# A fused attention and two-layer MLP kernel: the bank of the filling products is used as two halves of 256 columns

## The chip, the core and the metric

The kernel runs on one core of a Trainium2 chip. The metric is device time in microseconds (us) of one execution. TensorE is called PE, VectorE DVE, ScalarE ACT, GpSimd POOL; SyncE (SP) only starts transfers. PE multiplies a weight tile of 128x128 with a moving tile and adds the result up in PSUM, which has eight banks of 512 float32 columns per partition. ACT and DVE can read PSUM, POOL works on SBUF alone.

## The reference

Three steps follow each other, all in float32:

```
scores = q @ k^T / 8                      # 4 batches x 8 heads, 576 x 576, head size 64
scores = where(scores >= max - tau, scores, -1e9)
x = softmax(scores) @ v                   # gives x: 2304 tokens x 512
g = s * relu(x @ w_in)^2 + b              # w_in 512 x 2048
y = g @ w_out                             # w_out 2048 x 512
h = y @ w2_in                             # second layer, 512 x 2048
out = (max(h,0) + alpha * min(h,0)) @ w2_out
```

## The kernel before

A product of two float32 tiles is made of three fast products: each operand is split in a high and a low part, and `mm3` (lines 504 to 507) issues low x high, high x low and high x high into the same columns of PSUM. So every small step of the first layer is three matmuls, on lines 505, 506 and 507.

The work has four stages: attention (32 heads in 16 pairs), the first layer, and the two products of the second layer. A planner (class `Plan`) takes all tasks with their engine, an estimated time, the buffers that they take and a rank, runs through them in estimated time and writes each engine's instructions in the order that comes out. On the chip that order is fixed: an engine that meets an instruction whose input or buffer is not ready stands there, whatever lies behind it. The waits themselves are put in by the framework below the planner, from what each instruction reads and writes.

Attention leaves PE with gaps. They are filled with a part of the first layer, called the fill here: six blocks of 256 tokens, and of the 16 feature chunks of 128 the first 10 (`NA`). The fill has the lowest rank (`LATER + j`), so the planner issues three of its matmuls when no task of attention is ready. For one block the fill does this (lines 1011 to 1031):

- `load_x` reads 256 tokens of x back from memory and splits them (lines 518 to 524). A block waits here until attention has stored these tokens.
- `hidden` (lines 529 to 538) makes two feature chunks, 2 x 4 x 3 matmuls into the 512 columns of one bank.
- `square` (lines 540 to 558): ACT evicts the bank with a ReLU (line 543), then DVE (lines 548, 549) or POOL (551, 552) squares, ACT makes the high part (555), DVE or POOL the low one (556).
- After five such pairs come the outputs: two output chunks side by side in one bank, 2 x 10 x 3 matmuls, evicted by one ACT copy (line 1028) and stored to `ya`.

Of the eight banks, attention holds two double banks for scores (`sc`) and three single ones (`bank0` to `bank2`). The fourth single bank, `bank3`, is the fill's only one (`moe_s`, line 365); at the start the transposes of the first four pairs use it too (line 681). While a bank is being evicted the planner gives it to nobody, and issues tasks of attention on PE.

When attention has ended, `switch` (line 1036) frees its banks. What is left of the fill and then all other blocks of the first layer (six blocks of 384 tokens, `blocks_b`, lines 1086 to 1126) use them. That next stage starts on PE with products of the tile `xb`, which ACT and DVE make from x (lines 522 and 523).

## Time and profile before

| what | value |
|---|---|
| three timed runs | 1107.9, 1107.91, 1109.72 us; median 1107.91 |
| the profiled execution | 1105.83 us, its span 1104.0 us |
| PE busy | 1072.1 us, 97% of the span |
| DVE busy | 924.6 us, 84% |
| ACT busy | 749.3 us, 68% |
| POOL busy | 341.5 us, 31% |
| granted clock of PE | 0.997 of full speed over the span |

The span runs from the first to the last instruction. Attention and the fill take the first 507 us, and from there PE does the rest of the first layer and the second layer with hardly a gap. Matmuls overlap: one of 256 columns is shown with 0.28 us from start to end, but the next starts 0.12 us after it. So a short wait of PE does not show as idle time in full, and the starts tell more than the busy time.

### The profile page before, as it was taken

How to read it: one execution, taken by the hardware profiler on the slowest of the kernel's cores; microseconds unless marked ns; L12 is line 12 of the kernel's file. 1: busy time of each engine (PE TensorE's matmuls, PEld its weight loads, DVE VectorE, ACT ScalarE, POOL GpSimd, SP SyncE). 2: the span in 40 equal slices, each digit the busy share in tenths (PEclk: the TensorE clock that was granted, in tenths of full speed). 3: DMA queues.
4: the chain of work that ended last, by engine and by line, in shares of the span. 5: the costliest groups of instructions: out<-in, count | busy, mean ns of one | idle time of the engine just before them, and what ended most of it. 6: DMA issues, size and time to landing. Idle time of an engine off the chain costs nothing.

```text
span 1104.0 us, 22088 instructions
## 1 busy us (share of the span) xinstructions
PE 1072.1 (97%) x7536; PEld 1032.0 (93%) x7536; DVE 924.6 (84%) x2076; ACT 749.3 (68%) x1727; POOL 341.5 (31%) x466
## 2 busy tenths in 40 slices
PE   8899999999999999999999999999999999999998
PEld 6677889997999999989999999999999999999998
DVE  4899998989888889868877789589987999998882
ACT  4788877777868878754553467367787998565551
POOL 1466754544756647410000013010120332112111
PEclk8999999999999999999999999999999999999999
DMA  5646365436435453225376555348844474653531
GB/s 129 158 125 178 91 143 129 110 104 152 120 91 129 105 137 91 70 102 163 115 218 212 173 190 165 121 128 269 278 145 162 150 227 140 163 162 111 148 97 39
DMA packets 185264, 158.35 MB, mean 143 GB/s; under 512 B 72000, under 2 KB 162112, under 8 KB 185152
## 3 DMA queue, kind: packets, MB, share of 16 engines
q1 hardware_dynamic: 182624, 154.79, 49.2%
q10 hardware_dynamic: 2528, 2.16, 0.7%
q8 instruction: 59, 0.97, 0.4%
q14 instruction: 53, 0.43, 0.1%
HBM read 91.10 MB, written 44.56 MB: 123 GB/s over the span
## 4 chain that ended last, share of the span: by engine, by line
PE 75%; DVE 11%; ACT 5%; DMA 4%; issue 2%; SPq 1%; POOL 0%; DVEq 0%; ACTq 0%
PE bank L505 11%; PE bank L506 11%; PE bank L507 11%; PE bank_b L506 8%; PE bank_b L507 8%; PE bank_b L505 8%; PE bank L877 6%; PE sc L767 6%; PE bank L298 3%; PE bank L296 3%; DVE e L783 2%; DVE mx L777 1%; ACT e L781 1%; DMA stg<-xs 1%; SPq L645 1%
## 5 line engine op out<-in xcount | busy, mean ns | idle before, releaser
L783 DVE SCALAR_TENSOR_TENSOR e<-sc,mx,e 128x576 f32<-128x576 f32 x144 | 116.1, 812 | 13.0 <-ACT e L781 8.0
L781 ACT ACTIVATE e<-sc,mx 128x576 f32<-128x576 f32 x144 | 106.2, 742 | 19.5 <-DVE mx L777 19.0
L777 DVE TENSOR_REDUCE mx<-sc 128x1 f32<-128x576 f32 x144 | 106.8, 750 | 11.4 <-PE sc L767 10.6
L505 PE MATMUL bank<-gt,wa 128*128 128x256 f32 (+1 forms) x367 | 115.7, 315 | 0.5 <-ACT xr L1198 0.4
L506 PE MATMUL bank<-gt,wa 128*128 128x256 f32 (+1 forms) x367 | 110.3, 300 | 0.3 <-DVE gt L556 0.3
L507 PE MATMUL bank<-gt,wa 128*128 128x256 f32 (+1 forms) x367 | 110.3, 300 | 0.0
L298 PE MATMUL bank<-eyes,e 128*128 128x128 f32 (+1 forms) x320 | 90.3, 288 | 2.0 <-DVE e L783 1.9
L505 PE MATMUL bank<-xt,wa 128*128 128x256 f32 (+1 forms) x262 | 81.4, 311 | 3.8 <-ACT rest L543 3.2
L506 PE MATMUL bank<-xt,wa 128*128 128x256 f32 (+1 forms) x262 | 75.1, 287 | 0.0
L507 PE MATMUL bank<-xt,wa 128*128 128x256 f32 (+1 forms) x262 | 75.0, 286 | 0.0
L779 POOL TENSOR_SCALAR mx<-mx,tau_s 128x1 f32<-128x1 f32 x144 | 47.5, 331 | 81.8 <-DVE mx L777 78.3
L505 PEld LDWEIGHTS bank<-gt,wa 128*128 128x128 f32 x367 | 70.4, 192 | 1.2 <-ACT xr L1198 0.7
L506 PEld LDWEIGHTS bank<-gt,wa 128*128 128x128 f32 x367 | 69.5, 189 | 0.5 <-DVE gt L556 0.5
L507 PEld LDWEIGHTS bank<-gt,wa 128*128 128x128 f32 x367 | 69.4, 189 | 0.0
L767 PE MATMUL sc<-k,q 128*128 128x288 f32 x272 | 66.6, 371 | 2.7 <-DVE e L783 2.2
L877 PE MATMUL bank<-gl,vt 128*128 128x256 f32 (+1 forms) x192 | 63.6, 332 | 0.9 <-DVE gl L935 0.8
L877 PE MATMUL bank<-gh,vt 128*128 128x256 f32 (+1 forms) x192 | 57.9, 302 | 1.3 <-DVE gl L943 0.4
L505 PEld LDWEIGHTS bank<-xt,wa 128*128 128x128 f32 x262 | 50.6, 193 | 5.7 <-ACT rest L543 4.4
L767 PEld LDWEIGHTS sc<-k,q 128*128 128x128 f32 x272 | 44.9, 195 | 10.3 <-DVE e L783 3.8
L935 DVE TENSOR_TENSOR gl<-bank,gh 128x256 fp32r<-128x256 f32 (+1 forms) x96 | 43.3, 451 | 12.7 <-ACT gh L933 12.2
L566 ACT ACTIVATE gt<-rest,b_b,s_b 128x384 fp32r<-128x384 f32 x56 | 39.3, 705 | 21.0 <-DVE rest L564 20.6
L563 ACT ACTIVATE rest<-bank_b 128x384 f32<-128x384 f32 x39 | 19.1, 490 | 50.7 <-PE bank_b L507 50.6
(675 smaller groups left out, 4176.8 us busy)
## 6 DMA issues: line engine op xcount, KB each, us to landing
stg<-in_moe_w_in_dram SPq DMA_DIRECT2D x32, 512.0 KB, 4.1
stg<-in_moe_w_out_dram SPq DMA_DIRECT2D x32, 512.0 KB, 3.8
qo<-hq SPq DMA_DIRECT2D x32, 256.0 KB, 4.5
gf<-rest SPq DMA_DIRECT2D x34, 192.0 KB, 2.0
rest<-gf SPq DMA_DIRECT2D x46, 128.0 KB, 2.8
ko<-hk SPq DMA_DIRECT2D x32, 144.0 KB, 2.5
xr<-xs SPq DMA_DIRECT2D x6, 768.0 KB, 4.5
yf<-yb SPq DMA_DIRECT2D x24, 192.0 KB, 2.7
```

The source lines that it names most:

```text
L298: nc.tensor.transpose(to, part(x), one)
L505: nc.tensor.matmul(o, lhsT=wl, rhs=mh, start=first, stop=False, skip_group_check=on_top)
L506: nc.tensor.matmul(o, lhsT=wh, rhs=ml, start=False, stop=False, skip_group_check=on_top)
L507: nc.tensor.matmul(o, lhsT=wh, rhs=mh, start=False, stop=last, skip_group_check=on_top)
L566: t = add("ACT", act(n, 2, True), lambda: nc.scalar.activation(g.t[:, 0, :n], r.t[:, :n], AF.Identity, bias=b_b, scale=s_b), (r,), (g,), r ...
L767: nc.tensor.matmul(sp.t[:, x, :HS], lhsT=o[0][:, c], rhs=o[1][:, x * HS:(x + 1) * HS], start=n == 0, stop=n == len(passes) - 1)
L777: add("DVE", dve(S), lambda sp=sp, mx=mx: nc.vector.tensor_reduce(mx.t[:, 0:1], sp.t[:, :, :HS], op=ALU.max, axis=AX.XY, negate=True), (sp ...
L779: t2 = add("POOL", 0.26, lambda mx=mx: nc.gpsimd.tensor_scalar(mx.t[:, 1:2], mx.t[:, 0:1], -1.0, tau_s, op0=ALU.mult, op1=ALU.subtract), ( ...
L781: add("ACT", act(S, 1), lambda sp=sp, mx=mx, e=e: nc.scalar.activation(halves(e.t), sp.t[:, :, :HS], AF.Exp, bias=mx.t[:, 0:1]), (sp, mx), ...
L783: add("DVE", dve(S) + 0.065, lambda sp=sp, mx=mx, e=e, col=col, sums=sums: nc.vector.scalar_tensor_tensor(halves(e.t), sp.t[:, :, :HS], mx ...
L877: nc.tensor.matmul(o.t[:, :n], lhsT=w.rearrange("p a b -> p (a b)"), rhs=m.t[:, :n], start=c == first and x == 0, stop=c == last and x == ...
L935: add("DVE", dve(n), lambda hi=hi, lo=lo, gt=gt: nc.vector.tensor_tensor(lo.t[:, :n], gt.t[:, :n], f32(hi.t[:, :n]), op=ALU.subtract), (gt ...
```

## The change

The fill no longer takes `bank3` as a whole. When the last transposes of the first four pairs have been evicted, the bank is handed over as two halves of 256 columns (`half_s`), and from then on they stay with the fill until its end. A half holds one feature chunk of one block, or one output chunk. Each half is evicted by its own ACT instruction of 256 columns; the squaring that follows still works on two chunks at once. The first product of a block now comes after the last product of the block before (`full` is set behind each pair of output chunks). The banks that attention leaves go to the next stage alone, which gets `bank3` when the fill has ended.

```diff
--- before.py
+++ after.py
@@ -362,7 +362,8 @@
     banks = tiles(ps, 4, "bank", [P, 512])
     two_s = Slots(tiles(ps_att, 2, "sc", [P, 2, 512]))
     one_s = Slots(banks[:3], {"gt": 2, "o": 1, "misc": 1})
-    moe_s = Slots(banks[3:], {"h": 1})
+    whole_s, half_s, moe_s = Slots(banks[3:]), Slots(), Slots(caps={"h": 4})
+    of_whole = []
 
     def hwdge(fn, reads=(), writes=(), rank=None, kb=128, after=()):
         return add("SP", 0.6, fn, reads, writes, after, rank, tail=Plan.LAND + kb / 180.0)
@@ -526,21 +527,22 @@
         chain[0] = (t,)
         return xs
 
-    def hidden(xs, n, fs, units, rank, last=()):
-
-        h = Buf(moe_s, "h")
-        for i, f in enumerate(fs):
-            u = units[f // 2]
-            for c, x in enumerate(xs):
-                def go(i=i, f=f, c=c, x=x, u=u):
-                    mm3(h.t[:, i * n:(i + 1) * n], u.w_in(0, c, f), u.w_in(1, c, f), x.t[:, 0], x.t[:, 1], c == 0, c == NC - 1)
-                last = (add("PE", pe_r(n, 3), go, (x, u.buf), (h,), after=last, rank=rank),)
+    def hidden(xs, n, f, units, rank, last, slots):
+
+        h = Buf(slots, "h")
+        u = units[f // 2]
+        for c, x in enumerate(xs):
+            def go(c=c, x=x):
+                mm3(h.t[:, :n], u.w_in(0, c, f), u.w_in(1, c, f), x.t[:, 0], x.t[:, 1], c == 0, c == NC - 1)
+            last = (add("PE", pe_r(n, 3), go, (x, u.buf), (h,), after=last, rank=rank),)
         return h, last[0]
 
-    def square(h, n, r_slots, g_slots, others):
-
+    def square(hs, m, r_slots, g_slots, others):
+
+        n = m * len(hs)
         r, g = Buf(r_slots), Buf(g_slots)
-        add("ACT", act(n), lambda: nc.scalar.activation(r.t[:, :n], h.t[:, :n], AF.Relu), (h,), (r,), rank=SOON)
+        for i, h in enumerate(hs):
+            add("ACT", act(m), lambda i=i, h=h: nc.scalar.activation(r.t[:, i * m:(i + 1) * m], h.t[:, :m], AF.Relu), (h,), (r,), rank=SOON)
 
         def go(e):
             x = r.t[:, :n]
@@ -678,7 +680,7 @@
                     if s0:
                         tr = of_tails
                     else:
-                        tr = Buf(one_s, {"k": "misc", "q": "gt"}[nm]) if p == 0 and not tail else Buf(moe_s) if whole else Buf(one_s, "misc")
+                        tr = Buf(one_s, {"k": "misc", "q": "gt"}[nm]) if p == 0 and not tail else Buf(whole_s) if whole else Buf(one_s, "misc")
 
                         def transpose(t=t, tr=tr, cs=(NQ,) if tail else tuple(range(NQ))):
                             for i, c in enumerate(cs):
@@ -692,6 +694,7 @@
                         if nm == "k":
                             add("ACT", act(n), lambda hl=hl, tr=tr, c=c, n=n: nc.scalar.activation(
                                 k32[p][:, c], tr.t[:, :n], AF.Copy), (tr,), (hl,), rank=ready)
+                            of_whole.append(plan.tasks[-1])
                             continue
                         for h in range(2):
                             c0 = 2 * NQ * P + h * TL if tail else h * NQ * P
@@ -703,6 +706,7 @@
                                     nc.scalar.activation(q32[p][:, c], tr.t[:, of], AF.Copy, scale=sc_h[h])
 
                             add([("DVE", dve(n) + 0.065, ready), ("ACT", act(n, 1), ready)], 0, scaled, (tr,), (hl,))
+                            of_whole.append(plan.tasks[-1])
                         continue
                     if nm == "k":
                         x = add("ACT", act(n), lambda hl=hl, tr=tr, c=c, n=n: nc.scalar.activation(
@@ -1007,25 +1011,30 @@
             u1o[u] = Unit(w1o, "1o", u, W1O[0] + W1O[1] * u, early=True)
 
 
+        add("POOL", 0.01, lambda: half_s.add([banks[3][:, :TA], banks[3][:, TA:]]), after=of_whole, rank=-2.0)
         full = ()
         for j, (c0, n) in enumerate(blocks_a):
             x = load_x(xs, of_xs(c0, n), c0, n, stg_s, x_s, SOON, LATER)
             gs = []
             for f in range(0, NA, 2):
-                h, last = hidden(x, n, (f, f + 1), u1i, LATER + j, full)
-                gs.append(square(h, 2 * n, r_s, g_s, LATER if j + 2 < NJA else SOON))
+                hs = []
+                for i in range(2):
+                    h, last = hidden(x, n, f + i, u1i, LATER + j, full, half_s)
+                    full = (last,)
+                    hs.append(h)
+                gs.append(square(hs, n, r_s, g_s, LATER if j + 2 < NJA else SOON))
             for d in range(0, NC, 2):
-                y, t = Buf(moe_s), Buf(ysb_s)
+                t = Buf(ysb_s)
                 for i in range(2):
+                    y = Buf(half_s)
                     for f in range(NA):
                         def go(i=i, d=d, y=y, f=f, g=gs[f // 2], n=n):
                             u, c = u1o[f // 2], slice(f % 2 * n, (f % 2 + 1) * n)
-                            mm3(y.t[:, i * n:(i + 1) * n], u.w_out(0, f, (d + i) * P, P), u.w_out(1, f, (d + i) * P, P),
+                            mm3(y.t[:, :n], u.w_out(0, f, (d + i) * P, P), u.w_out(1, f, (d + i) * P, P),
                                 g.t[:, 0, c], g.t[:, 1, c], f == 0, f == NA - 1)
                         last = add("PE", pe_r(n, 3), go, (gs[f // 2], u1o[f // 2].buf), (y,), after=(last,), rank=LATER + j)
-                        if f == 0 and i == 0:
-                            full = (last,)
-                add("ACT", act(2 * n), lambda y=y, t=t: nc.scalar.activation(t.t, y.t, AF.Copy), (y,), (t,), rank=SOON)
+                    add("ACT", act(n), lambda y=y, t=t, i=i, n=n: nc.scalar.activation(t.t[:, i * n:(i + 1) * n], y.t[:, :n], AF.Copy), (y,), (t,), rank=SOON)
+                full = (last,)
                 hwdge(lambda t=t, d=d, c0=c0, n=n: nc.sync.dma_start(
                     ya[d * P:(d + 2) * P, c0:c0 + n].rearrange("(c p) t -> p c t", p=P), t.t.rearrange("p (c t) -> p c t", c=2)),
                     (t,), (ya_d[j][d // 2],), SOON, 256)
@@ -1046,7 +1055,6 @@
             xb_s.add(late["xb"])
             ps_b = ctx.enter_context(tc.tile_pool(name="ps_b", bufs=1, space=PSUM))
             moe_s.add(banks[:3] + tiles(ps_b, 4, "bank_b", [P, 512]))
-            moe_s.caps["h"] = 4
 
         sw = add("POOL", 0.01, switch, after=of_attention, rank=-2.0)
         of_a = plan.tasks[:]
@@ -1055,6 +1063,7 @@
             xb_s.add(cut(xt, TB))
             gb_s.add(cut(gt, TB))
             rb_s.add(rt)
+            moe_s.add(banks[3:])
 
         add("POOL", 0.01, switch_b, after=of_a, rank=-2.0)
 
@@ -1094,7 +1103,7 @@
 
             def first(f):
                 seq[0] += 1e-4
-                h, full[0] = hidden(x, n, (f,), u1i, seq[0], (full[0],))
+                h, full[0] = hidden(x, n, f, u1i, seq[0], (full[0],), moe_s)
                 return square_b(h, n, rb_s, gb_s)
 
             def second(f, g):
```

The lines of the changed kernel are a few higher: `mm3` is on 506 to 508, the scores on 771, the products with v on 881, the ReLU on 545, the copy of an output chunk on 1036.

Three places show how the instructions are moved. `bank_106` to `bank_109` are `bank0` to `bank3`; a wait names the engine whose instruction is waited for. First PE, in the third block of the fill, at the third feature pair (`wa_90` holds the weights of the second pair, `wa_91` those of the third, `xt` the block's x). Before:

```order
L505 MATMUL bank_109<-xt,wa_90 128x256
L506 MATMUL bank_109<-xt,wa_90 128x256
L507 MATMUL bank_109<-xt,wa_90 128x256
L767 MATMUL sc_110<-ko_1287,qo_1285 128x288 [waits DMAHW7_49,DMAHW6_49,DVE_49]
L767 MATMUL sc_110<-ko_1287,qo_1285 128x288 x3
L296 MATMUL bank_106<-eyes_r,e0r 128x128 [waits DVE_49]
L298 MATMUL bank_106<-eyes,e_144 128x128
L505 MATMUL bank_109<-xt,wa_91 128x256 [waits Activation_49]
```

Now:

```order
L881 MATMUL bank_106<-gl_1295,vt_1286 128x320 [waits DVE_49]
L881 MATMUL bank_106<-gh_1290,vt_1286 128x320 [waits Activation_49]
L506 MATMUL bank_109<-xt,wa_91 128x256
L507 MATMUL bank_109<-xt,wa_91 128x256
L508 MATMUL bank_109<-xt,wa_91 128x256
...
L506 MATMUL bank_109<-xt,wa_91 128x256 [waits Activation_49]
...
L771 MATMUL sc_110<-ko_1284,qo_1282 128x288 [waits DVE_49]
L771 MATMUL sc_110<-ko_1284,qo_1282 128x288 x3
L296 MATMUL bank_108<-eyes_r,e0r 128x128
```

Before, the wait for the eviction stands at the first product of the next pair, with scores and transposes of attention ahead of it. Now a product under way in one half waits for the eviction of the other half, with products of the same half right ahead of it.

Second PE again, from the last product of attention to the first of the next stage. Before:

```order
L877 MATMUL bank_107<-gl_1295,vt_1289 128x320
L877 MATMUL bank_107<-gh_1292,vt_1289 128x320
L505 MATMUL bank_109<-xt,wa_91 128x256
...
L505 MATMUL bank_109<-xt,wa_93 128x256
...
L505 MATMUL bank_106<-gt,wa_94 128x256
...
L505 MATMUL bank_108<-xb_5928,wa_89 128x384
```

Now:

```order
L881 MATMUL bank_106<-gl_1294,vt_1287 128x320
L881 MATMUL bank_106<-gh_1290,vt_1287 128x320
L506 MATMUL bank_109<-gt,wa_96 128x256
...
L506 MATMUL bank_109<-gt,wa_98 128x256
...
L506 MATMUL bank_106<-xb_6062,wa_89 128x384
```

Before, 186 matmuls of the fill are left there, with feature products (`xt`) among them; now 108, all of them of the last block's outputs (`gt`).

Third ACT, at the end of the fill. Before:

```order
L543 ACTIVATE rest<-bank_109 128x512
L555 ACTIVATE gt<-rest 128x512
L522 ACTIVATE xb_5928<-xr_5919 128x384
L522 ACTIVATE xb_5929<-xr_5919 128x384
L522 ACTIVATE xb_5930<-xr_5919 128x384
L522 ACTIVATE xb_5931<-xr_5919 128x384
```

Now:

```order
L1036 ACTIVATE rest<-bank_109 128x256 x3
L523 ACTIVATE xb_6062<-xr_6053 128x384
L523 ACTIVATE xb_6063<-xr_6053 128x384
L1036 ACTIVATE rest<-bank_109 128x256
L523 ACTIVATE xb_6064<-xr_6053 128x384
L523 ACTIVATE xb_6065<-xr_6053 128x384
```

Before, the tiles of the next stage are made while the last feature pairs are evicted; now they stand behind three of the last four evictions of the fill, two of them behind the last.

## Rows read from the trace of the kernel before

**Rows 1.** The page: busy time by engine; PE and its clock in 40 slices.
```profile
PE 1072.1 (97%) x7536; PEld 1032.0 (93%) x7536; DVE 924.6 (84%) x2076; ACT 749.3 (68%) x1727; POOL 341.5 (31%) x466
...
PE   8899999999999999999999999999999999999998
...
PEclk8999999999999999999999999999999999999999
```

**Rows 2.** Busy time by stretch; columns are named in the first line.
```profile
core 0: us, PE busy (x) PEld busy (x) DVE busy (x) ACT busy (x) POOL busy (x), PEclk, DMA share, GB/s
102.00:254.00 152.00, 145.77 (x1154) 136.23 (x1153) 136.01 (x299) 117.39 (x259) 83.14 (x114) 1.00 0.46 113
254.00:400.00 146.00, 141.66 (x1173) 135.88 (x1172) 128.27 (x301) 112.10 (x258) 85.82 (x125) 1.00 0.52 125
400.00:482.00 82.00, 80.53 (x679) 78.29 (x678) 69.31 (x158) 63.27 (x144) 46.25 (x68) 1.00 0.31 76
```

**Rows 3.** Chain of waits by line, of 102:254, 254:400 and 400:482, in turn.
```profile
by line: PE bank L877 15.3%; PE sc L767 11.6%; PE bank L505 8.3%; PE bank L507 7.9%; PE bank L506 7.9%; PE bank L298 6.1%; PE bank L296 5.9%; DVE e L783 5.5%; DVE mx L777 4.6%; ACT e L781 3.6%; issue 3.4%; DMA xs<-z 2.9%; DMA stg<-xs 2.4%; 
by line: PE sc L767 11.4%; PE bank L877 10.4%; PE bank L505 7.9%; PE bank L506 7.6%; PE bank L507 7.6%; PE bank L298 6.5%; DVE e L783 6.4%; PE bank L296 6.1%; DMA stg<-xs 4.2%; issue 4.1%; DVE mx L777 3.0%; DMA qo<-hq 2.7%; ACT e L781 2.6%;
by line: PE bank L877 15.7%; PE sc L767 14.4%; PE bank L505 13.7%; PE bank L506 12.6%; PE bank L507 12.6%; PE bank L298 8.9%; PE bank L296 8.6%; DVE e L783 1.8%; issue 1.4%; DVE gl L935 1.3%; DVE rc L816 1.3%; ACT rest L543 1.2%; DVE gt L55
```

**Rows 4.** Timeline of PE and ACT: an eviction with nothing else on PE.
```profile
483.61 0.28 PE L506 MATMUL bank<-xt,wa 128*128 128x256 f32 x1
483.73 0.28 PE L507 MATMUL bank<-xt,wa 128*128 128x256 f32 x1
484.70 0.38 PE L505 MATMUL bank<-xt,wa 128*128 128x256 f32 x1 [0.69 <-ACT rest L543]
...
484.05 0.60 ACT L543 ACTIVATE rest<-bank 128x512 f32<-128x512 f32 x1 [1.38 <-PE bank L507]
```

**Rows 5.** Groups by line and form, 100 to 507 us.
```profile
L933 ACT ACTIVATE gh<-bank 128x256 fp32r<-128x256 f32 x48 | 18.5, 385 | 3.2 <-PE bank L298 2.4 <-DVE gh L929 0.3
L543 ACT ACTIVATE rest<-bank 128x512 f32<-128x512 f32 x30 | 17.9, 598 | 8.3 <-PE bank L507 8.0
L551 POOL TENSOR_TENSOR rest<-rest 128x512 f32<-128x512 f32 x14 | 14.7, 1051 | 4.7 <-ACT rest L543 4.6
L548 DVE SCALAR_TENSOR_TENSOR rest<-rest,s_b 128x512 f32<-128x512 f32 x16 | 13.6, 852 | 5.6 <-ACT rest L543 5.4
L552 POOL TENSOR_SCALAR rest<-rest,s_b,b_b 128x512 f32<-128x512 f32 x14 | 10.8, 771 | 1.5
L549 DVE TENSOR_SCALAR rest<-rest,b_b 128x512 f32<-128x512 f32 x16 | 8.3, 519 | 0.6
```

**Rows 6.** Timeline of PE: work of attention between two products of the fill.
```profile
332.43 0.28 PE L877 MATMUL bank<-gl,vt 128*128 128x256 f32 x1
332.55 0.28 PE L877 MATMUL bank<-gh,vt 128*128 128x256 f32 x1
332.67 0.22 PE L296 MATMUL bank<-eyes_r,e0r 128*128 128x128 f32 x1
332.73 0.23 PE L296 MATMUL bank<-eyes_r,e1r 128*128 128x128 f32 x1
...
339.49 0.69 PE L767 MATMUL sc<-ko,qo 128*128 128x288 f32 x4
340.02 0.28 PE L505 MATMUL bank<-xt,wa 128*128 128x256 f32 x1
```

**Rows 7.** What PE waited for, 102 to 507 us: us in total, times, longest.
```profile
PE bank L505 <- ACT rest L543: 3.2, 5, 0.8
PE bank L505 <- ACT rest L1028: 0.6, 2, 0.4
```

**Rows 8.** Timeline of PE: attention's last products; the next stage's first.
```profile
481.40 0.31 PE L877 MATMUL bank<-gl,vt 128*128 128x320 f32 x1
481.55 0.31 PE L877 MATMUL bank<-gh,vt 128*128 128x320 f32 x1
...
506.59 0.34 PE L505 MATMUL bank<-xb,wa 128*128 128x384 f32 x1
506.76 0.34 PE L506 MATMUL bank<-xb,wa 128*128 128x384 f32 x1
```

**Rows 9.** Tile xr, 480 to 512 us: ns min/median/max, first and last start.
```profile
L522 ACT ACTIVATE xb<-xr x5: 505/509/526, 494.2 to 501.5; 128x384 fp32r<-128x384 f32 x5
L523 DVE TENSOR_TENSOR xb<-xr,xb x5: 551/553/559, 495.0 to 502.1; 128x384 fp32r<-128x384 f32 x5
```

**Rows 10.** The page's costliest groups: the softmax of attention.
```profile
L783 DVE SCALAR_TENSOR_TENSOR e<-sc,mx,e 128x576 f32<-128x576 f32 x144 | 116.1, 812 | 13.0 <-ACT e L781 8.0
L781 ACT ACTIVATE e<-sc,mx 128x576 f32<-128x576 f32 x144 | 106.2, 742 | 19.5 <-DVE mx L777 19.0
L777 DVE TENSOR_REDUCE mx<-sc 128x1 f32<-128x576 f32 x144 | 106.8, 750 | 11.4 <-PE sc L767 10.6
```

## The prediction

> **What bounds the kernel now.** I read the page first: PE is busy for 97% of the span, at the full clock of 2.4 GHz nearly throughout [rows 1], and the change neither adds nor removes a matmul (7,370 in the program before and after). So the time can move only where PE waits, and from 507 us on it hardly does. Next the stretches in which the fill runs [rows 2]: PE is idle for 6.2, 4.3 and 1.5 us of 152, 146 and 82 us, while DVE is busy for 89, 88 and 85%. Two engines are close to full, so I asked the chain of waits, by stretch, whose delay is the kernel's [rows 3]. Adding up PE's lines, the chain stands on PE for 63% of the first stretch, 58% of the second and 86% of the third. That is the share I use below: a microsecond lost by PE costs that much of itself.
>
> **What an eviction costs PE.** Where nothing else stands between the last product of a pair and the next product into the same bank, the starts are 483.73 and 484.70, 0.97 us apart against 0.12 us between products that follow each other [rows 4]: 0.85 us are lost. ACT's read of 512 columns is 0.60 us of it. With 256 columns the nearest row is an eviction of attention, 0.385 against 0.598 us [rows 5], so a turnaround of a half should cost 0.85 - 0.21 = 0.64 us. Work of attention between the two products takes its own time off this: 0.12 us a product with v, 0.06 us a transpose, 0.53 us for a score of four matmuls [rows 6].
>
> **Part 1, halves that are not free of each other.** The planner treats the two halves as two buffers. The order of the changed kernel has waits that it knows nothing of: a product in one half waits for the eviction of the other half, and this eviction waits for products of the neighbour that stand ahead of it in the order. In 57 of the fill's 84 evictions it is a half-made neighbour that is stopped like this. The trace of before has no such case, since each of its evictions takes a whole bank and the next product into it has to wait anyway.
>
> The Trainium skill speaks of this on the page PSUM — Partial Sum Buffer, section "PSUM bank collisions raise a hardware error": two engines must not be on one bank (of the same partitions) at the same time, whichever columns they touch, and semaphores should guard banks, not addresses. By that rule the waits are needed, and halving a bank gives no second buffer; without them the 84 evictions would cost about 1.5 us instead of the 22.8 us below, and the sum would come out some 15 us lower. The waits in the order agree with the rule; no run here shows the chip without them.
>
> I went through both orders and gave each eviction its price less the attention work that stands between, never below zero. Before: 40 evictions have a later product into bank3; 3 have nothing between, 17 less than 0.85 us; 6.4 us in all. (The trace shows 3.8 us of it as idle time, in 7 waits [rows 7]; with the 0.16 us by which a matmul's end lies behind its successor's start, 7 times, 4.9 us.) Now: 84 evictions, 24 with nothing between, 49 with less than 0.64 us; 22.8 us in all. By place:
>
> - blocks 1 and 2 (the first stretch): 2.6 before, 7.6 now, +5.0; times 0.63 gives +3.1 us
> - blocks 3 and 4 (the second): 0.8 and 6.2, +5.4; times 0.58 gives +3.1 us
> - from there to the last product of attention: 0.7 and 7.1, +6.4; times 0.86 gives +5.5 us
> - behind attention, where PE has nothing else: 2.3 and 1.9, -0.3 us
>
> Together +11.4 us. Its bounds: 0 if every one falls into time in which PE waits anyway, and 16.4 us if none does. Queued behind a stopped product are attention's scores and transposes, and DVE waits for these (L777, L783).
>
> **Part 2, fill that moves forward.** With a half free more often, the planner puts more of the fill into attention: behind attention's last product 108 matmuls are left instead of 186. In the trace that tail takes from 481.55 to 506.59 us [rows 8]; 78 matmuls of 0.12 us are 9.4 us less of it. They are a gain only where they go into time that PE spent waiting. All of it is the upper bound (9.4 us); the lower is the chain's word on the third stretch, where most of them go: 14% off PE, so 1.3 us. The planner does place them where no task of attention was ready, and the page shows 12 us of idle PE over the three stretches before short waits are added, so I take two thirds: -6.3 us.
>
> **Part 3, smaller terms.** ACT gets 42 more instructions, each pair costing 2 x 0.385 - 0.598 = 0.17 us more, 7.2 us in all. It is busy for 77% of these stretches [rows 2] and on the chain for about 3% [rows 3]: +0.3 us; if it were as critical as DVE, +0.7 us. Seven of the 30 squarings go from DVE (0.85 + 0.52 us) to POOL (1.05 + 0.77 us) [rows 5]: 9.6 us less for DVE, which has about a tenth of the chain: -1.0 us, with 0 and -2 as bounds; POOL, busy for 57%, has room for 12.7 us. The start of the next stage: two of its four first tiles now stand on ACT behind the fill's last eviction. This one can start about 0.3 us after the last product of the fill, ends at 0.7, and the third tile's high and low parts follow at 1.2 and 1.8 us (0.51 and 0.55 us [rows 9]). PE takes 3 x 0.17 us a tile [rows 8], wants the third tile's high part at 1.0 and its low part at 1.2 us, and so stands for 0.6 us: +0.6 us, between 0 and 1.5. One block behind the other costs nothing: with one bank a block could not start before the outputs of the last were evicted either. The hand-over at the start costs nothing: the fill's first product stands at the same place in PE's order.
>
> **The sum.** 11.4 - 6.3 + 0.3 - 1.0 + 0.6 = +5.0 us. The profiled execution took 1105.83 us (span 1104.0), which gives 1110.8 us; the median of the timed runs lies 2.1 us above it, and by that scale I forecast 1112.9 us.
>
> **Rivals.**
>
> - Faster: PE's other waits take the turnarounds in. Attention's end is then set by DVE (maximum, mask and sum of the scores take 0.75 and 0.81 us of it a tile [rows 10], and it is 85 to 89% busy), so a PE that comes late is not missed, and the whole tail of 9.4 us is won. For it: DVE's load in the first two stretches. Against it: 86% of the chain on PE in the third. With a quarter of part 1 left (+3), the full -9.4 and the small terms: about -6.5 us, 1101.4 us. It decides where part 1 reaches the end for less than 9.5 us while the tail's 9.4 us are won in full.
> - No change. Part 1 as worked out, and part 2 won in full: 11.4 - 9.4 - 0.1 = +1.9 us, 1109.8 us, the upper edge of what can't be told from none. For it: the planner moves the fill only to where no task of attention was ready. Against it: on the chip a turnaround that the planner does not know shifts PE against its plan, and the gap it meant to fill may be over.
> - Slower by more. An eviction waits not for PE alone: if ACT is in attention's exponential of 0.74 us [rows 10] when the half is ready, PE stands for what is left of it. Half of 0.74 us on the 24 turnarounds with nothing between gives 8.9 us, times some 0.7 is 6 us more: +11, 1119 us. For it: the planner places these evictions by a clock that PE no longer keeps. Against it: before, ACT starts its eviction within some 0.04 us of a matmul's shown end where that is what it waits for, as at 484.05 [rows 4].
>
> **How the numbers follow.** Forecast 0.40, faster 0.25, no change 0.20, slower by more 0.15. Differences below 0.2% (2.2 us) can't be told from none. The forecast's own spread, from the bounds of parts 1 and 2, is 1108 to 1116 us; a few of its cases fall within 0.2%, and a few of the no-change cases come out slower, which leaves 0.25 faster, 0.20 the same, 0.55 slower. The range goes down to the faster rival (1101) and up past the slower one (1121).
>
> **What would show it.** Right: PE waits for the ReLU and the output copy some 30 times or more and for 8 us or more of idle time, against 7 times and 3.8 us; the starts around such a wait lie about 0.76 us apart; the time from attention's last product to the next stage's first is about 15 us instead of 25; attention's last product comes 10 to 16 us later than at 481.55. Wrong: attention's last product comes less than 9 us later, or the waits cost PE far less than 0.64 us each. If the next stage and those behind it took a different time (PE's order there is nearly the same, and its waits few), the forecast would be right or wrong by accident.

## The result, and the profile after

The changed kernel takes 1123.0 us (median of 4 runs, 1121.9 to 1124.3), the kernel before beside it 1108.3 us (4 runs, 1107.9 to 1109.7): ratio 1.0131, 95% interval 1.0114 to 1.0149, or 14.7 us more. I forecast 1112.9 us in a range from 1101 to 1121. The sign is right; the size is three times the +5.0 us I worked out, and the time lies outside the range.

The profiled execution took 1123.63 us, with a span of 1121.6. It lies 17.8 us above the profiled execution of before, which was 2.1 us faster than its own median; so what is read below from this pair of traces adds up to some 3 us more than the 14.7 us between the medians. Its page, the busy times that answer to [rows 1]:

```profile
PE 1080.3 (96%) x7536; PEld 1034.5 (92%) x7536; DVE 914.8 (82%) x2056; ACT 763.5 (68%) x1781; POOL 344.9 (31%) x474
...
PEclk9999999999999999999999999999999999999999
```

The engines did the same work, so the time is in waits. What PE waited for up to the next stage, 102 to 524 us (us in total, times, longest), which answers to [rows 7]; L545 is the ReLU, L1036 the output copy:

```profile
PE bank L506 <- ACT rest L545: 10.5, 26, 0.5
PE bank L506 <- ACT rest L1036: 4.0, 10, 0.5
PE sc L771 <- DVE e L787: 1.5, 3, 0.8
```

There are 36 waits for an eviction with 14.5 us of idle time, where there were 7 with 3.8 us. One of them in the timeline of PE and then of ACT, beside [rows 4]: a feature product (`xt`) stopped by the eviction of an output in the other half.

```profile
342.96 0.28 PE L507 MATMUL bank<-xt,wa 128*128 128x256 f32 x1
343.08 0.28 PE L508 MATMUL bank<-xt,wa 128*128 128x256 f32 x1
343.83 0.38 PE L506 MATMUL bank<-xt,wa 128*128 128x256 f32 x1 [0.47 <-ACT rest L1036]
...
343.40 0.38 ACT L1036 ACTIVATE rest<-bank 128x256 f32<-128x256 f32 x1 [0.32 <-PE bank L508]
```

The starts are 0.75 us apart, of which 0.12 is the usual spacing: 0.63 us lost. ACT in its turn stood idle for 0.32 us until the product ahead had ended. That side of the coupling grew too. What ACT waited for at its evictions up to attention's last product, after (102 to 508.5 us) and then before (102 to 481.5 us):

```profile
ACT rest L545 <- PE bank L508: 17.0, 39, 1.2
ACT rest L1036 <- PE bank L508: 5.8, 14, 0.8
```

```profile
ACT rest L543 <- PE bank L507: 4.0, 8, 0.8
ACT rest L1028 <- PE bank L507: 1.1, 2, 0.7
```

Whatever stands behind such an eviction in ACT's queue waits with it: 22.8 us in 53 waits against 5.1 in 10. Behind attention's last product either kernel has another 11 us of such waits, where ACT has little else to do.

The chain of waits in the three stretches of [rows 3]:

```profile
by line: PE bank L881 16.0%; PE sc L771 14.6%; PE bank L506 12.7%; PE bank L508 10.6%; PE bank L507 10.5%; PE bank L298 7.3%; PE bank L296 6.6%; DMA stg<-in_moe_w_out_dram 3.8%; DMA qo<-hq 3.3%; ACT rest L545 2.6%; issue 2.1%; ACT e L785 1.
by line: PE sc L771 14.8%; PE bank L881 13.9%; PE bank L506 13.9%; PE bank L507 11.8%; PE bank L508 11.8%; PE bank L298 8.8%; PE bank L296 7.8%; DMA qo<-hq 3.5%; DVE e L787 2.4%; ACT rest L545 2.3%; ACT e L785 1.8%; issue 1.7%; DVE mx L781 
by line: PE bank L506 17.0%; PE sc L771 14.5%; PE bank L881 14.4%; PE bank L508 13.8%; PE bank L507 13.6%; PE bank L298 8.7%; PE bank L296 7.9%; ACT rest L545 2.9%; ACT rest L1036 2.3%; DVE rest L550 2.2%; issue 1.4%; ACT gh L937 0.5%; DVE 
```

PE's lines add up to 78, 83 and 90%; they were 63, 58 and 86%. The share that I used as a weight was that of the old order; in the new one PE is on the chain for more of the first two stretches, and ACT's evictions have joined it.

The end of attention, beside [rows 8] (timeline of PE):

```profile
508.57 0.31 PE L881 MATMUL bank<-gh,vt 128*128 128x320 f32 x1
...
523.89 0.34 PE L506 MATMUL bank<-xb,wa 128*128 128x384 f32 x1
```

Attention's last product is 27.0 us later, the tail 15.3 us instead of 25.0, and the next stage starts 17.3 us later. Behind that nothing more is lost (span +17.6).

One thing I had not priced stands in the middle. The third block of the fill needs an x that attention makes. PE's last fill product before that block and the first of it, after, then before:

```profile
249.23 0.29 PE L508 MATMUL bank<-gt,wa 128*128 128x256 f32 x1
...
276.65 0.36 PE L506 MATMUL bank<-xt,wa 128*128 128x256 f32 x1
```

```profile
254.03 0.29 PE L507 MATMUL bank<-gt,wa 128*128 128x256 f32 x1
...
268.56 0.36 PE L505 MATMUL bank<-xt,wa 128*128 128x256 f32 x1
```

27.4 us without fill instead of 14.5; this is the dry stretch of what follows. It begins 4.8 us earlier and ends 8.1 us later. Busy times in these two stretches, after and then before (columns as in [rows 2]):

```profile
249.35:276.60 27.25, 21.36 (x141) 17.68 (x140) 22.63 (x53) 18.67 (x46) 11.56 (x19) 0.94 0.57 140
```

```profile
254.15:268.55 14.40, 12.59 (x86) 9.84 (x85) 14.10 (x34) 12.45 (x32) 6.89 (x11) 1.00 0.66 164
```

139 matmuls of attention stand between the two products, not 84 (the rows also count the ends of two fill products): the fill moved ahead of them and then had nothing to do while they ran at attention's own pace. That x comes late, too: its DMA into `xs` is issued at 265.23 instead of 256.31 us. And PE's clock fell in the stretch (0.94 in the row above; before it was 1.00), after some 8 us with gaps in PE's work. Within it:

```profile
258.00:260.00 2.00, 2.00 (x11) 1.98 (x11) 1.12 (x2) 1.07 (x2) 0.44 (x2) 0.50 0.67 140
```

PE ran at 1.2 GHz for about 3.4 us, busy nearly throughout; by that, an estimate, some 1.7 us of the stretch are the clock's.

**An account of PE.** For every start of a matmul I took the distance to the one before it, less the usual spacing of its kind (0.12 us for a product of the fill). What is left over I sorted by what stood there: an eviction of the fill, the dry stretch at the third block, anything else from 98.5 us on. In us, up to the next stage's first product (what is missing to the sum is the time until 98.5 us and the usual spacings themselves). Each row is one execution; the executions of one kernel differ by 1 to 5 us, so differences of that size in the last column are not the change's for sure:

| kernel | evictions | dry stretch | other waits | attention's last product | tail | next stage at |
|---|---|---|---|---|---|---|
| before | 5.1 | 6.2 | 49.2 | 481.55 | 25.0 | 506.59 |
| changed | 20.9 | 13.4 | 42.4 | 508.57 | 15.3 | 523.89 |
| e1_planned | 13.6 | 4.1 | 52.2 | 473.78 | 40.4 | 514.16 |
| e2_split | 9.4 | 5.9 | 55.3 | 488.64 | 28.6 | 517.22 |
| e9_pe_before | 5.1 | 6.3 | 45.0 | 495.13 | 26.9 | 522.07 |
| e10_act_small | 5.0 | 2.1 | 55.5 | 476.92 | 31.6 | 508.52 |
| e11_free | 7.5 | 4.1 | 51.9 | 473.67 | 34.2 | 507.92 |
| e12_hold | 3.7 | 6.2 | 59.7 | 481.22 | 33.5 | 514.76 |
| e13_told | 4.8 | 2.8 | 51.2 | 474.52 | 30.0 | 504.54 |

The +17.3 us of the changed kernel are +15.8 at evictions, +7.2 in the dry stretch, -6.8 in other waits, +1.5 before the fill starts, -0.4 in spacings.

### The profile page after: what moved, and what is told of

It is laid out like the page before. It is cut to its first block, busy times and chain, and to the rows that moved or that the text cites. A ratio compares the mean times of both kernels' runs of the same rounds, so it can differ in the third digit from the quotient of the medians.

```text
span 1121.6 us, 22148 instructions
## 1 busy us (share of the span) xinstructions
PE 1080.3 (96%) x7536; PEld 1034.5 (92%) x7536; DVE 914.8 (82%) x2056; ACT 763.5 (68%) x1781; POOL 344.9 (31%) x474
## 4 chain that ended last, share of the span: by engine, by line
PE 83%; DVE 6%; ACT 5%; DMA 3%; issue 2%; SPq 1%; DVEq 0%; ACTq 0%
PE bank L506 14%; PE bank L508 13%; PE bank L507 13%; PE bank_b L507 8%; PE bank_b L508 8%; PE bank_b L506 8%; PE sc L771 7%; PE bank L881 7%; PE bank L298 3%; PE bank L296 3%; DVE e L787 1%; ACT rest L545 1%; ACT e L785 1%; DVE mx L781 1%; DMA stg<-in_moe_w_out_dram 1%
## 5 line engine op out<-in xcount | busy, mean ns | idle before, releaser
L787 DVE SCALAR_TENSOR_TENSOR e<-sc,mx,e 128x576 f32<-128x576 f32 x144 | 116.3, 812 | 16.0 <-ACT e L785 14.1
L781 DVE TENSOR_REDUCE mx<-sc 128x1 f32<-128x576 f32 x144 | 107.1, 751 | 18.7 <-PE sc L771 17.6
L506 PE MATMUL bank<-gt,wa 128*128 128x256 f32 (+1 forms) x316 | 98.4, 311 | 4.5 <-ACT rest L1036 3.2
L506 PE MATMUL bank<-xt,wa 128*128 128x256 f32 (+1 forms) x276 | 88.8, 322 | 10.5 <-ACT rest L545 9.4
L508 PE MATMUL bank<-gt,wa 128*128 128x256 f32 (+1 forms) x316 | 93.1, 295 | 0.0
L507 PE MATMUL bank<-gt,wa 128*128 128x256 f32 (+1 forms) x316 | 93.0, 294 | 0.0
L508 PE MATMUL bank<-xt,wa 128*128 128x256 f32 (+1 forms) x276 | 79.8, 289 | 0.0
L507 PE MATMUL bank<-xt,wa 128*128 128x256 f32 (+1 forms) x276 | 79.7, 289 | 0.0
L506 PEld LDWEIGHTS bank<-xt,wa 128*128 128x128 f32 x276 | 53.0, 192 | 17.5 <-ACT rest L545 15.0
L506 PEld LDWEIGHTS bank<-gt,wa 128*128 128x128 f32 x316 | 60.5, 191 | 7.2 <-ACT rest L1036 5.3
L507 PEld LDWEIGHTS bank<-gt,wa 128*128 128x128 f32 x316 | 59.8, 189 | 0.0
L508 PEld LDWEIGHTS bank<-gt,wa 128*128 128x128 f32 x316 | 59.7, 189 | 0.0
L507 PEld LDWEIGHTS bank<-xt,wa 128*128 128x128 f32 x276 | 52.3, 190 | 0.3
```

Of the source, the lines that this page charges most:

```text
L506: nc.tensor.matmul(o, lhsT=wl, rhs=mh, start=first, stop=False, skip_group_check=on_top)
L507: nc.tensor.matmul(o, lhsT=wh, rhs=ml, start=False, stop=False, skip_group_check=on_top)
L508: nc.tensor.matmul(o, lhsT=wh, rhs=mh, start=False, stop=last, skip_group_check=on_top)
L781: add("DVE", dve(S), lambda sp=sp, mx=mx: nc.vector.tensor_reduce(mx.t[:, 0:1], sp.t[:, :, :HS], op=ALU.max, axis=AX.XY, negate=True), (sp ...
L787: add("DVE", dve(S) + 0.065, lambda sp=sp, mx=mx, e=e, col=col, sums=sums: nc.vector.scalar_tensor_tensor(halves(e.t), sp.t[:, :, :HS], mx ...
```

## The experiments

Theory 1 was made after the result: it takes the prediction's turnarounds that the planner doesn't know, but counts them in full and gives the moved fill nothing. The rivals are named in the expectations. Each time stands beside runs of the kernel before on the same chip (1107.2 to 1108.3 us); a difference to the changed kernel is taken across chips, on which the kernel before differs by up to 1 us. The edits are cut to their main lines.

**e1_planned.** The changed kernel, its planner told that the halves are one bank: no product starts while an eviction of either is due or running, and no eviction behind a product under way.

```diff
...
+                    if t.part == "product" and evicting or t.part == "evict" and now < until:
+                        held.append(item)
+                        continue
...
```

> The changed kernel, with a planner that knows the bank: while an eviction of one half is due or runs, no product of the fill is issued into the other half, and an eviction starts only behind the product under way. Turnarounds counted in its order as before: 12.1 us (13 with nothing between), against 22.8 (24) in the changed kernel and 6.4 (3) in the one before; 240 matmuls of the fill are left behind attention. Theory 1 (each turnaround that stands in the order without other work is lost in full, and fill that moves forward wins nothing): 6.4 + 5.7 as against before, so about 1114 us. Rival (halves or the 42 extra ACT instructions cost by themselves, planned or not): it stays above 1120 us.

1113.4 us, ratio 1.005 (1.0034 to 1.0066). What PE waited for, 102 to 524 us (lines 11 higher):

```profile
PE bank L517 <- ACT rest L556: 8.0, 16, 0.9
PE bank L517 <- ACT rest L1047: 2.3, 3, 1.4
```

Inside attention 3.5 us are left of the 18.4 lost at evictions. But the planner now holds the fill back, and the tail of 40.4 us pays for most of what is left. By the two ratios, 0.8 of the 1.3%, some 9 us, go when the planner knows the bank. Not all of it need be the waits themselves: the order is another elsewhere too, and the dry stretch is 8.5 us long instead of 27.4.

**e2_split.** The kernel before, a whole bank evicted by two ACT instructions of 256 columns, the planner told.

```diff
...
+            for o in (0, n // 2):
+                nc.scalar.activation(r.t[:, o:o + n // 2], h.t[:, o:o + n // 2], AF.Relu)
...
+        add("ACT", 2 * act(n // 2), relu, (h,), (r,), rank=SOON)
...
```

> The kernel before, whole bank, each eviction made of two ACT instructions of 256 columns one behind the other; so it has the 42 extra ACT instructions of the change and none of its halves. Theory 1: turnarounds grow by 0.17 us to 1.02 us where they show; counted in its order they are 10 to 13 us instead of 6.4, so 1111 to 1114 us. Rival (the extra ACT work is what costs): near the changed kernel, over 1118 us.

1115.4 us, 1.0071 (1.0055 to 1.0087), 8.1 us more. The starts around an eviction with nothing else are 1.03 us apart. Evictions account for +4.3, other waits for +6.1: more than half of what is lost here isn't at the bank.

**e3_dup_after, e4_dup_before.** Every eviction done twice, the planner not told.

```diff
-        add("ACT", act(n), lambda: nc.scalar.activation(r.t[:, :n], h.t[:, :n], AF.Relu), (h,), (r,), rank=SOON)
+        add("ACT", act(n), lambda: [nc.scalar.activation(r.t[:, :n], h.t[:, :n], AF.Relu) for _ in range(2)], (h,), (r,), rank=SOON)
...
```

> The changed kernel, same order on PE, each eviction of a half made twice (the second ACT instruction writes the same values again; the planner is not told). A turnaround grows from 0.64 to 1.03 us; counted in the order the sum goes from 22.8 to 44.4 us, +21.6 us. Theory 1: nearly all of it reaches the end, +18 to +22 us, 1141 to 1145 us. Rival, the chain share of the prediction (0.7): +15 us, 1138 us. Rival (PE's waits take them in): under +8 us, below 1131 us.

> The kernel before, same order on PE, each eviction of the whole bank made twice, planner not told. A turnaround grows from 0.85 to 1.45 us; counted in the order the sum goes from 6.4 to 20.6 us, +14.2 us. Theory 1: +12 to +15 us, 1120 to 1123 us: a kernel with a whole bank gets as slow as the changed one by turnarounds alone. Rival (chain share 0.7): +10 us. Rival (waits take them in): under +5 us.

1150.5 us (1.0386, 1.0364 to 1.0409), 27.5 over the changed kernel; and 1128.9 us (1.019, 1.0175 to 1.0205), 21.6 over the kernel before. Both are more than I expected. What PE waited for in e3, 102 to 540 us:

```profile
PE bank L506 <- ACT rest L545: 24.6, 36, 1.2
PE bank L506 <- ACT rest L1036: 8.1, 12, 0.9
```

These two mix a longer turnaround with ACT's time; e7 and e8 take them apart.

**e7_act_before, e8_act_after.** As e4 and e3, but the second instruction copies the evicted tile onto itself in SBUF: the bank is free after the first.

```diff
+        add("ACT", act(n), lambda: [nc.scalar.activation(r.t[:, :n], x[:, :n], AF.Relu) for x in (h.t, r.t)], (h,), (r,), rank=SOON)
...
```

> The kernel before, same order on PE; each eviction is followed by a second ACT instruction that copies the evicted tile in SBUF onto itself: the same load on ACT as the doubled eviction (+25 us), but the bank is free after the first. Theory 1 (the bank's turnaround is what counts): at most +6 us, 1108 to 1113 us, against +21.6 us for the doubled eviction. Rival (ACT's load counts): +15 us or more, over 1122 us.

> The changed kernel with the same edit: +35 us of ACT in 84 instructions, no turnaround longer. Theory 1: at most +8 us over the changed kernel, 1123 to 1131 us, against 1150 us for the doubled eviction. Rival (ACT's load counts): 1140 us or more.

1125.9 us (1.0162, 1.0141 to 1.0184) and 1133.1 us (1.023, 1.0209 to 1.025): 18.7 over the kernel before and 10.1 over the changed one. Theory 1 allowed 6 and 8 us; in e7 the rival holds, e8 lies between the two. ACT time behind the planner's back costs without the bank: in e7 the evictions lose 1.4 us more, other waits 17.6 more. So most of e4 is not the bank. What of it is ACT's queue and what the evicted tile, which the squaring gets later by the same copy, these two runs don't part. In the changed kernel, with the same order, e3 less e8 leaves 17.4 us for turnarounds longer by one ACT read.

**e5_x0_before, e6_x0_after.** Every block of the fill reads the x of the first 256 tokens, so that no block waits for attention; the first layer's results of the other tokens are left out of the fill.

```diff
-            x = load_x(xs, of_xs(c0, n), c0, n, stg_s, x_s, SOON, LATER)
+            x = load_x(xs, of_xs(0, n), 0, n, stg_s, x_s, SOON, LATER)
```

> The kernel before, but each of the six blocks of the fill reads the first 256 tokens of x instead of its own (that part of the output is left out), so no block waits for attention to store its x. 168 matmuls of the fill are left behind attention instead of 186, and the turnarounds counted in its order are 10.3 us instead of 6.4. Both theories: PE no longer stands dry between the second and third block (the gap of 13.9 us between 254.65 and 268.56), worth 0 to 6 us: 1102 to 1108 us.

> The changed kernel with the same edit. Nothing of the fill is left behind attention (168 matmuls in the run it is compared with), and the turnarounds counted are 26.3 us, 16.0 us more than there. Theory S (fill that moves forward won nothing in the changed kernel because the fill ran dry at the third block's x): with x at hand the 20 us moved forward pay, and it is at most 6 us slower than the run it is compared with. Theory 1 (turnarounds reach the end in full; moving the fill forward wins nothing where PE is the bound): 14 to 18 us slower than that run.

1107.8 us (1.0002, 0.9993 to 1.0012) and 1137.9 us (1.027, 1.0252 to 1.0288), 30.1 apart, against 14 to 18 by theory 1 and at most 6 by theory S. (The 13.9 us of the first expectation run from 254.65 us; the fill's last product starts at 254.03, so the gap is 14.5 us.) What PE waited for in e6, 102 to 536 us:

```profile
PE bank L506 <- ACT rest L545: 12.6, 32, 0.5
PE bank L506 <- ACT xb L523: 9.3, 1, 9.3
PE bank L881 <- POOL vt L740: 4.5, 1, 4.5
```

The evictions lose 24.5 us against 7.8 in e5: +16.7, again the full count. 13.8 us more are two single stops, one of them at the next stage's first tile, which comes too late for a fill that ends early. The rest of the other waits falls by 2.1 us, with PE at half clock for some microseconds behind each stop. So the turnarounds cost as much without the dry stretch; what the fill would win without it can't be read from this pair, since the stops are new.

**e9_pe_before.** The kernel before, the first matmul of each of the 84 chunks issued three times: 20.2 us more of PE, the planner not told.

```diff
...
+                    if c == 0 and n == TA:
+                        again(h.t[:, i * n:(i + 1) * n], u.w_in(1, c, f), x.t[:, 0])
...
```

> The kernel before with 168 more matmuls on PE: the first one of each of the fill's 120 groups of sums... counted by chunks, 60 feature and 24 output chunks, is issued three times (it overwrites, so the values stay), and the planner is not told. 168 x 0.12 = 20.2 us of work for PE, 2.2 us of it behind attention's last product; nothing else is changed, ACT has the same load and no turnaround is longer. Theory P (PE is the bound of attention with its fill, and whatever PE does or loses there reaches the end in full): +18 to +21 us, 1125 to 1128 us. Chain share of the prediction (0.58 to 0.86): +14 us, 1121 us. Rival (PE's waits take it in): under +10 us.

1121.9 us, 1.0128 (1.0111 to 1.0145): +14.1 us, 0.70 of the work. Added PE work costs what the chain's shares say, and the theory that everything on PE costs one for one falls.

**e10_act_small, e13_told.** The kernel before; 0.17 us of ACT behind each eviction, planned. In e10 it is a copy of 96 columns in SBUF; in e13 nothing is issued, and only the order is that of e10.

```diff
...
+        add("ACT", act(96, 0, True), lambda: None, (r,), (r,), after=(t,), rank=SOON)
...
```

> The kernel before with 42 more ACT instructions of about 0.17 us (96 columns of each evicted tile copied onto themselves in SBUF), and the planner told: the same 7.2 us for ACT as the halves bring, no turnaround longer; counted in its order the turnarounds are 7.2 us instead of 6.4. If ACT's load is what the changed kernel pays for: +5 us or more, 1112 us. If it is the turnarounds: at most +2 us, 1107 to 1109 us.

> The kernel of the small ACT instructions without them: the planner still counts 0.17 us behind each eviction, so every engine has that kernel's order, with 216 matmuls of the fill left behind attention instead of 186 and ACT's load as before. If the order is what was faster there: 1100 to 1104 us, 4 to 7 us faster than the kernel before. If the instructions helped (by giving ACT's next eviction a later place): 1106 us or more.

1103.4 us (0.9964, 0.9952 to 0.9976) and 1102.7 us (0.9955, 0.9938 to 0.9971). Between the two lie 0.7 us, less than either's spread, so no cost of the planned ACT time can be told; the gain is the order's. e13 beats both kernels, by 5.2 us the one before. In its profile the dry stretch is 4.1 us long instead of 14.5, and the next stage starts 2.1 us earlier; the profiled span is 3.7 us shorter, and I didn't follow where the rest comes from.

**e11_free.** e1, with the first 256 columns of the three banks that attention leaves given to the fill for its tail.

```diff
...
+            half_s.free[:0] = [t[:, :TA] for t in banks[:3]]
...
```

> The planned halves of the first experiment, and behind attention the fill also gets the first 256 columns of the three banks that attention leaves, so that its tail needs no turnaround. In the first experiment attention ended at 473.78 us, 7.8 us earlier than before, and the tail took 40.4 us for 240 matmuls (28.8 us). Turnarounds counted in this order: 6.9 us instead of 12.1. Theory P: the tail falls to 30 us, so about 1113.4 - 9 = 1104 us, 3 us faster than the kernel before. Rival (attention only looked faster because its work stood differently; halves cost by themselves): 1109 us or more.

1107.4 us, 0.9996 (0.9987 to 1.0006): the tail falls from 40.4 to 34.2 us, and the kernel is as fast as before. With the planner knowing the bank, halves neither win nor lose; the 1104 us I hoped for did not come.

**e12_hold.** The kernel before, the fill's last block held until attention's last product is placed.

```diff
+            if j == NJA - 1:
+                full = (*full, *[t for t in of_attention if t.ways[0][0] == "PE"])
```

> The kernel before, whole bank, with the last block of the fill held until attention's last product: 240 matmuls are left behind attention instead of 186, that is 54 (6.5 us) moved back out of attention, the opposite of what the change moves. Turnarounds counted in its order: 5.0 us instead of 6.4. Theory P (PE is the bound: attention ends earlier by what is taken out of it, whatever moves over its end wins or costs nothing): attention ends about 6 us earlier, the whole within 2 us of the kernel before, 1106 to 1110 us. The prediction's part 2 (two thirds of what moves forward is won, so two thirds of what moves back is lost): 4 us slower or more, 1112 us.

1113.3 us, 1.005 (1.0032 to 1.0067): 5.0 us slower, so fill at the end of attention does go into time that PE would wait: with 6.5 us of it taken out, attention's last product came only 0.3 us earlier (481.22), not about 6. Not all of it is that, since the clock fell. Busy times of e12 by stretch (columns as in [rows 2]):

```profile
470.00:474.00 4.00, 2.92 (x21) 2.23 (x19) 2.76 (x9) 2.94 (x10) 1.60 (x3) 1.00 0.19 66
...
477.00:478.00 1.00, 0.56 (x4) 0.43 (x4) 0.49 (x1) 0.00 (x0) 0.00 (x0) 1.00 0.00 0
...
479.00:480.00 1.00, 0.65 (x3) 0.35 (x3) 0.27 (x1) 0.32 (x1) 0.66 (x1) 0.53 0.00 0
480.00:484.00 4.00, 3.74 (x16) 3.75 (x17) 1.66 (x3) 0.56 (x2) 0.20 (x1) 0.50 0.00 0
...
486.00:488.00 2.00, 1.31 (x11) 1.11 (x11) 0.84 (x2) 0.60 (x1) 0.00 (x0) 1.00 0.57 127
```

From about 479 to 486 us PE ran at 1.2 GHz, and its fill products there start 0.21 us apart instead of 0.12: 21 of them, 2 us of the 8.2 by which the next stage is later in this pair of traces.

## Why the prediction was wrong in size

- **Turnarounds: counted right.** I counted 22.8 us against 6.4, +16.4; the account has +15.8. With nothing else in between one costs 0.63 us (0.64 predicted), the starts are 0.75 us apart (0.76), there are 36 waits (30 or more), and the loss leaves when the planner knows the bank (e1, e11).
- **Moved fill: the step that failed.** I put part 2 at -6.3 us. Other waits did fall, by 6.8 us. But I looked only at where the moved matmuls go in, not at where they are missing: the fill reaches its third block earlier and runs dry there for 27.4 instead of 14.5 us. That gives back 7.2 us, some 1.7 of them by the lower clock there. It is the order's doing: e3 and e8, with the changed kernel's order, have 28.4 and 28.1 us there, e7 and e9, with the order before, 15.1 and 14.5, though all four are slower than the kernel they were made from. The tail is as short as predicted (15.3 us), and nothing of it is left on net. That the 7.2 us reach the end in full is read from the account; the pair that was to show it, e5 and e6, has new stops.
- **The weight by the chain's share: 5.0 us too much off.** With it, turnarounds were to shrink from 16.4 to 11.4 us because PE's other waits would take some in, and the fill to win 6.3 beside that: 11.3 us together. All that other waits gave is 6.8, so 4.5 us are missing. The share is right for added PE work (e9: 0.70). Why a turnaround costs more is not settled; one difference is that it holds ACT as well (22.8 us of waits for PE inside attention against 5.1), and ACT held up costs by itself (e7). How the 6.8 us divide between the weight and the fill no run tells. Nor is the line between these 6.8 and the 7.2 us sharp: the 55 matmuls that the dry stretch has more stood among the other waits before. What is firm is the sum of both steps: PE's waits outside evictions were to fall by 11.3 us, and with the dry stretch they grew by 0.4.
- **ACT +0.3, squarings -1.0, hand-over +0.6.** e10 and e13 bear out that planned ACT time costs next to nothing. The other two were not tried alone. The premise that no matmul is added holds: the page counts 7536 before and after (the prediction's 7,370 stands on no page). The next stage follows the last fill product at the usual 0.12 us in the trace after, so the 0.6 us did not come.
- **In sum**, 12.3 us more than forecast up to the next stage: 7.2 dry stretch, 4.5 weight, 1.5 in the start (where the two kernels do the same), less 0.9 in the small terms and the count. Between the medians it is 9.7 us: about 3 of the 12.3 belong to the pair of executions, the 1.5 of the start perhaps among them.
- **Attention's last product** came 27.0 us later, not 10 to 16: 9.4 of moved fill, 15.1 of turnarounds inside attention, 2.5 the rest. I had let it keep only the weighted part.
- **Rivals.** Faster and no change fall, as PE's waits took in too little of the turnarounds (the other waits fell by 6.8 us, and the dry stretch took that back). The third, ACT busy when a half is ready, named the right direction for another reason: the longest wait is 0.5 us, no longer than a plain turnaround's.
- **The rule** on the page PSUM — Partial Sum Buffer of the Trainium skill (section "PSUM bank collisions raise a hardware error") describes what the trace shows: PE and ACT take turns on the bank, whichever half each is at. That the chip needs it no run here shows.

That the products no longer overlap changes nothing by itself: with one whole bank, that edit leaves the program as it was, instruction by instruction, since the last outputs have to be evicted first anyway.

## What to carry to other kernels

Two halves of one PSUM bank, one being written by PE while ACT reads the other, are not two buffers: here an eviction with no other work in between stopped the neighbour for 0.63 us, and PE waited at 36 of 84 evictions. Tell the planner such a rule, or count its waits at full price. When filler work moves forward, follow it to the next input that it needs before booking the shorter tail, and count what stands between in the new order (139 matmuls for 84): such a gap can be seen before the run.

## What the runs showed that I had not expected

- ACT time that the order does not know costs even where ACT is busy for 68% of the span: 42 extra copies in SBUF, which also hold up the squaring, 18.7 us (e7); with 7.2 us of ACT time that is planned the kernel is within 0.7 us of the same order without it (e10 and e13).
- An order alone is worth about 5 us either way (e12, where the lower clock is a part of it, and e13), as much as the whole effect I had forecast.
- PE's clock can fall where attention runs without fill. In the changed kernel it was 0.50 from 258 to 261 us of the dry stretch. In e12 it went to 0.50 after some 9 us in which PE was busy for about 70%; in e6 behind the stop of 9.3 us it was still 0.51 from 536 to 540 us, with PE busy all the time, and at 1.00 from 540 to 546. It need not: in the kernel before it stayed at 1.00 through 14.4 us without fill.
